# Layer-norm statistics of one slab moved to VectorE and of another to an earlier time on ScalarE, with their transposes at the head of the gate steps

## The chip, the cores and the metric

One core of a Trainium2 chip. The metric is device time of one execution in microseconds (us), median over runs on the chip. The span in a profile is about 1.8 us shorter than that time (185.5 against 187.29 in the first profile), because it runs from the first to the last instruction. The 193.67 of the kernel before is slow.

The engines: PE is the tensor engine (PEld its weight loads), DVE is VectorE, ACT is ScalarE, POOL is GpSimd, SP is the engine whose queue issues most transfers.

## The reference, cut to what matters

```python
xn = layernorm(x)                       # x: 2048 tokens x 512, bf16
h[t] = Lam_bar * h[t-1] + B_bar @ xn[t] # complex state of 512
s = 2 * Re(C @ h) + xn * Dskip
g = silu((gelu(xn @ w_gate) * (xn @ w_up)) @ w_down)   # hidden width 1376
out = x + s * g
```

## The kernel before

The 2048 tokens are four slabs of 512. For each slab PE computes eleven gate/up steps (`ffn`), then the scan's input for the next slab (`u_pair`, twice), then four tiles of the down projection (`down`). The products of the state with C (`y_mm`) for slab s are woven into the gate steps of slab s+1. The scan with its rotations runs on VectorE. PE needs the normalised input transposed; for slabs 1 to 3 ScalarE normalises a tile and a transposing transfer turns it:

```python
def ln_act(s, m):                       # statistics on ScalarE: sum and sum of squares
    for i, f in enumerate((AF.Copy, AF.Square)):
        junk = work.tile([P, D], BF16, name="junk", tag="junk", bufs=1)
        ACT(out=junk[:], in_=x_tok[:, s * M + m, :], func=f, accum_out=sx[:, s, i, m : m + 1])

def ln_out(s, m):                       # normalise on ScalarE, transpose by transfer
    xn = work.tile([P, D], BF16, name="xn", tag="xn", bufs=4)
    ACT(out=xn[:], in_=x_tok[:, s * M + m, :], func=AF.Identity, scale=rs[...], bias=nb[...])
    nc.sync.dma_start_transpose(out=xnT[:, :, c0 : c0 + P], in_=xn[:])

def epi(s, m, y_ps, g2):                # output tile: two VectorE operations, then the store
    ...
    nc.sync.dma_start(out=out_td[mg : mg + P, :], in_=ot[:])
```

Transposes and stores share one queue, SP's, which issues in program order. The order in slabs 1 and 2:

```python
if s < NS - 1:
    if j < M:           ln_act(s + 1, j)       # gate steps 0..3: statistics
    if j == M - 1:      ln_small(s + 1)        # four small VectorE ops, two on GpSimd
    if 5 <= j < 5 + M:  ln_out(s + 1, j - 5)   # gate steps 5..8: normalise and transpose
if j in Y_AT:                                  # Y_AT = (5, 7, 9, 10): y product and store
    m = Y_AT.index(j)
    epi(s - 1, m, y_mm(s - 1, m, hsts[s - 1]), g2s[s - 1, m])
```

The prologue, which turns out to matter for reading the times, runs idle matmuls (`dummies`) until the first normalised tiles are there:

```python
dummies(9)
nc.tensor.transpose(pt_ps[:, :], pv[:, :], ident[0:16, 0:16])
dummies(5)
...
tps = [t_xn0(0, xs[0]), t_xn0(1, xs[1])]       # first real work of PE
```

## Time and profile before

| | kernel before |
|---|---|
| runs ahead of the change | 187.57, 188.12, 193.67 us |
| profiled run | 187.29 us, span 185.5 us |
| PE busy | 178.7 us (96%) |
| VectorE busy | 151.6 us (82%) |
| ScalarE busy | 116.0 us (63%) |
| PE waits after 8.5 us | one, of 0.6 us |

How to read it: busy shares say which engine to look at; the waits say what it stood for; the chain says which of those stretches add up to the span. PE at 96% with one listed wait leaves little room. The lines are in the prediction below.

### The profile page before, as it was taken

What the parts mean: (1) busy time and instruction counts of PE and PEld (TensorE: products, weight loads), DVE (VectorE), ACT (ScalarE), POOL (GpSimd) and SP (SyncE); (2) the same over time, 40 slices, a digit from 0 to 9 for tenths busy, and PEclk for the clock granted to TensorE, in tenths of its full rate; (3) what the DMA queues carried; (4) which work ended last, traced back from release to release, by engine and by line L of the source; (5) the groups of instructions that cost most, each with busy time, mean ns of one, the idle gap of its engine ahead of it and who ended that gap; (6) DMA issues with size and microseconds to landing.
All of it is one profiled execution on the core that took longest, in us unless ns stands there. A gap on an engine that the chain in (4) does not pass through costs nothing.

```text
span 185.5 us, 2504 instructions
## 1 busy us (share of the span) xinstructions
PE 178.7 (96%) x887; PEld 85.8 (46%) x903; DVE 151.6 (82%) x233; ACT 116.0 (63%) x212; POOL 23.8 (13%) x42
## 2 busy tenths in 40 slices
PE   7899999999999999999999999989999999999992
PEld 2564444444444445444444444544444444554452
DVE  4877999999996699999999999999999993332034
ACT  3299996678899996376269949547329633441210
POOL 3679606200000110000000040000000000000000
PEclk9999999999999999999999999999999999999999
DMA  5996834895000013200000003300000000000001
GB/s 150 315 314 102 228 68 88 242 241 194 0 0 0 0 34 82 57 28 28 0 4 0 0 0 88 84 31 30 0 0 0 4 0 28 28 32 30 28 28 57
DMA packets 24444, 12.26 MB, mean 66 GB/s; under 512 B 15760, under 2 KB 24432, under 8 KB 24432
## 3 DMA queue, kind: packets, MB, share of 16 engines
q1 hardware_dynamic: 24256, 12.03, 25.8%
q8 instruction: 7, 0.11, 0.3%
q10 hardware_dynamic: 176, 0.07, 0.1%
q14 instruction: 5, 0.04, 0.1%
HBM read 6.33 MB, written 2.10 MB: 45 GB/s over the span
## 4 chain that ended last, share of the span: by engine, by line
PE 84%; ACT 6%; DVE 4%; DMA 3%; issue 1%; POOL 0%
PE f_ps L471 20%; PE up_ps L226 18%; PE g_ps L226 17%; PE u_ps L371 13%; PE y_ps L486 13%; ACT gt L459 2%; PE y_ps L491 2%; ACT ub L460 2%; DMA xnT<-xn 1%; DVE st L154 1%; DMA x_tok<-in_A_x_dram 1%; ACT xn L559 1%; PE y_ps L519 1%; DVE xn L165 1%; ACT L459 1%
## 5 line engine op out<-in xcount | busy, mean ns | idle before, releaser
L226 PE MATMUL g_ps<-xnT,wg 128*128 128x512 bf16 (+2 forms) x179 | 44.8, 369 | 0.8 <-ACT xnT L195 0.7
L226 PE MATMUL up_ps<-xnT,wu 128*128 128x512 bf16 (+2 forms) x181 | 45.2, 370 | 0.3
L471 PE MATMUL f_ps<-wd,at 128*128 128x512 bf16 (+1 forms) x172 | 38.5, 379 | 0.2
L459 ACT ACTIVATE gt<-g_ps 128x512 bf16<-128x512 f32 (+1 forms) x44 | 26.6, 605 | 11.6 <-PE g_ps L226 9.3
L460 ACT ACTIVATE ub<-up_ps 128x512 bf16<-128x512 f32 (+1 forms) x44 | 26.8, 610 | 4.3 <-PE up_ps L226 4.3
L417 DVE TENSOR_TENSOR_SCAN Ft<-rho,it,Wt 128x512 bf16<-128x512 f32 x24 | 29.3, 1266 | 0.0
L371 PE MATMUL u_ps<-xnT,BT 128*128 128x512 bf16 x127 | 28.4, 379 | 0.7 <-DMA xnT<-xn 0.6
L486 PE MATMUL y_ps<-C,hst 128*128 128x512 bf16 x117 | 28.2, 379 | 0.2
L226 PEld LDWEIGHTS <-wu 128*128 128x128 bf16 (+1 forms) x184 | 18.3, 100 | 19.7
L471 PEld LDWEIGHTS <-at 128*128 128x128 bf16 (+1 forms) x176 | 17.1, 98 | 20.6
L226 PEld LDWEIGHTS <-wg 128*128 128x128 bf16 (+1 forms) x184 | 17.8, 100 | 18.4 <-issue 0.8
L376 ACT ACTIVATE U<-u_ps 128x512 bf16<-128x512 f32 x32 | 19.0, 616 | 11.6 <-PE u_ps L371 11.6
L476 ACT ACTIVATE g<-f_ps 128x512 f32<-128x512 f32 x16 | 9.6, 597 | 22.6 <-PE f_ps L471 22.6
L504 DVE TENSOR_TENSOR yg<-y_ps,g 128x512 bf16<-128x512 f32 x15 | 10.2, 682 | 14.1 <-PE y_ps L491 10.3
L464 DVE TENSOR_TENSOR at<-gt,ub 128x1024 bf16<-128x1024 bf16 x20 | 13.7, 684 | 9.8 <-ACT ub L460 9.8
L371 PEld LDWEIGHTS <-BT 128*128 128x128 bf16 x128 | 12.4, 98 | 15.5 <-issue 0.9
L486 PEld LDWEIGHTS <-hst 128*128 128x128 bf16 x120 | 11.7, 98 | 13.6
L554 POOL TENSOR_TENSOR rs<-sx,mhalf 128x4 f32<-128x4 f32 x2 | 3.2, 1594 | 72.6 <-DVE sx L551 42.2
L559 ACT ACTIVATE xn<-x_tok,nb,rs 128x512 bf16<-128x512 bf16 x12 | 10.2, 849 | 2.9 <-POOL nb L555 2.9
L391 DVE TENSOR_TENSOR Wt<-pp,qq 128x1024 bf16<-128x1024 bf16 x16 | 10.5, 688 | 0.3
L391 DVE TENSOR_TENSOR hst<-pp,qq 128x1024 bf16<-128x1024 bf16 x16 | 10.4, 686 | 0.2
L387 DVE TENSOR_TENSOR pp<-U,cos_b 128x2048 bf16<-128x2048 bf16 x8 | 9.8, 1222 | 0.7 <-ACT U L376 0.4
(106 smaller groups left out, 159.8 us busy)
## 6 DMA issues: line engine op xcount, KB each, us to landing
out_dram<-ot SPq DMA_DIRECT2D x15, 128.0 KB, 1.7
x_tok<-in_A_x_dram SPq DMA_DIRECT2D x3, 512.0 KB, 6.6
wd<-in_B_w_down_dram SPq DMA_DIRECT2D x1, 1280.0 KB
wg<-in_B_w_gate_dram SPq DMA_DIRECT2D x1, 640.0 KB
wu<-in_B_w_up_dram SPq DMA_DIRECT2D x1, 640.0 KB, 8.6
wg<-in_B_w_gate_dram SPq DMA_DIRECT2D x1, 384.0 KB, 3.7
wu<-in_B_w_up_dram SPq DMA_DIRECT2D x1, 384.0 KB
wg<-in_B_w_gate_dram SPq DMA_DIRECT2D x1, 352.0 KB
```

The costliest lines, as they stand in the source:

```text
L226: nc.tensor.matmul(ps[:fs, a:b], lhsT=w[:, kt, fsl], rhs=xnT[:, kt, s * TS + a : s * TS + b], start=(kt == 0), stop=(kt == KT - 1),)
L371: nc.tensor.matmul(u_ps[:, :], lhsT=BT[:, ri, kt, pt * P : (pt + 1) * P], rhs=xnT[:, kt, cols], start=(kt == 0), stop=(kt == KT - 1),)
L376: ACT(out=U[:, ri, q, :], in_=u_ps[:, :], func=AF.Copy)
L391: return lambda: TT(out=dst()[i], in0=box["pp"][:, i, :, :], in1=box["qq"][:, 1 - i, :, :], op=op)
L417: nc.vector.tensor_tensor_scan(out=box["F"][:, ri, q, :], data0=rho[:, pt : pt + 1].to_broadcast([P, TS]), data1=box["W"][:, ri, q, :], in ...
L459: ACT(out=gt[:fs, i, :], in_=g_ps[:fs, :], func=AF.Gelu_apprx_tanh)
L460: ACT(out=ub[:fs, i, :], in_=u_ps[:fs, :], func=AF.Copy)
L464: dve(now() + 0.9, 0.61, lambda: TT(out=at[:, j - 1 : j + 1, :], in0=gt[:], in1=ub[:], op=ALU.mult))
L471: nc.tensor.matmul(f_ps[:, :], lhsT=at[:fs, k, m0 : m0 + P], rhs=wd[:fs, k, :], start=(k == 0), stop=(k == NFT - 1))
L486: nc.tensor.matmul(y_ps[:, :], lhsT=hst[:, j // NPT, j % NPT, m0 : m0 + P], rhs=C2[:, j // NPT, j % NPT, :], start=(j == 0), stop=False,)
L504: TT(out=yg[:], in0=y_ps[:, :], in1=g2[:], op=ALU.mult)
L559: ACT(out=xn[:], in_=x_tok[:, s * M + m, :], func=AF.Identity, scale=rs[:, s, m : m + 1], bias=nb[:, s, m : m + 1])
```

## The change

The intent: take the statistics passes of slabs 2 and 3 out of ScalarE's gate steps. Slab 2's go to VectorE, which has idle time early in slab 0; slab 3's stay on ScalarE but move under slab 1's down projection. The transposes can then go into gate steps 1 to 4. Slab 2's input is loaded earlier for this. A copy in the prologue is split over two engines, and the gate products are placed a little later in VectorE's order.

```diff
     load_gu(1)
+    load_x(2)
...
-    xnT_out(nc.scalar, 1, tps[1])
+    xnT_out(nc.scalar, 1, tps[1], 0, KT // 2)
+    xnT_out(nc.vector, 1, tps[1], KT // 2, KT)
...
+        lag = 0.9 + (2.5 if s == 0 else 0.5)
-            dve(now() + 0.9, 0.61, lambda: TT(out=at[:, j - 1 : j + 1, :], ...))
+            dve(now() + lag, 0.61, lambda: TT(out=at[:, j - 1 : j + 1, :], ...))
...
+    dve(13.0, 2.8, lambda: ln_vector(2))
...
+                if j == 3:
+                    ln_vector_small(2)
...
-                    for x in range(2, NS):
-                        load_x(x)
+                    load_x(3)
...
-                if s < NS - 1:
-                    if j < M:
-                        ln_act(s + 1, j)
-                    if j == M - 1:
-                        ln_small(s + 1)
-                    if 5 <= j < 5 + M:
-                        ln_out(s + 1, j - 5)
+                if s < NS - 1 and 1 <= j < 1 + M:
+                    ln_out(s + 1, j - 1)
...
+                if s == 1:
+                    ln_act(3, m)
+            if s == 1:
+                ln_small(3)
```

More of the change, by code (lines that the diff above doesn't have):

```diff
@@ L191, with xnT_out @@
     ACT(out=pf[:], in_=pt_ps[:, :], func=AF.Copy)
-    def xnT_out(eng, m, tp):
-        o = xnT[:, :, m * P : (m + 1) * P]
+    def xnT_out(eng, m, tp, k0=0, k1=KT):
+        o = xnT[:, k0:k1, m * P : (m + 1) * P]
         if eng is nc.scalar:
-            ACT(out=o, in_=tp[:, :, :], func=AF.Copy)
+            ACT(out=o, in_=tp[:, k0:k1, :], func=AF.Copy)
         else:
-            eng.tensor_copy(out=o, in_=tp[:, :, :])
+            eng.tensor_copy(out=o, in_=tp[:, k0:k1, :])
     bn(0, 0)
@@ L460, in ffn @@
         ACT(out=ub[:fs, i, :], in_=u_ps[:fs, :], func=AF.Copy)
+        lag = 0.9 + (2.5 if s == 0 else 0.5)
         if j == NFT - 1:
-            dve(now() + 0.9, 0.34, lambda: TT(out=at[:fs, j, :], in0=gt[:fs, 0, :], in1=ub[:fs, 0, :], op=ALU.mult))
+            dve(now() + lag, 0.34, lambda: TT(out=at[:fs, j, :], in0=gt[:fs, 0, :], in1=ub[:fs, 0, :], op=ALU.mult))
         elif i:
-            dve(now() + 0.9, 0.61, lambda: TT(out=at[:, j - 1 : j + 1, :], in0=gt[:], in1=ub[:], op=ALU.mult))
+            dve(now() + lag, 0.61, lambda: TT(out=at[:, j - 1 : j + 1, :], in0=gt[:], in1=ub[:], op=ALU.mult))
     def down(s, m, at):
@@ L566, with ln_vector, ln_vector_small @@
     hsts, ats, g2s = {0: hst0}, {0: at0}, {}
-    def ln1_stats():
+    G = nc.gpsimd
+    def ln_vector(x):
         for m in range(M):
-            bn(1, m)
+            bn(x, m)
         for m in range(M):
-            bn_end(1, m)
-    dve(10.3, 2.8, ln1_stats)
-    G = nc.gpsimd
-    ve1 = consts.tile([P, M], FP32, name="ve1")
-    G.tensor_scalar(out=ve1[:], in0=mv[:, 1, :, 1], scalar1=EPS, scalar2=None, op0=ALU.add)
-    G.tensor_tensor(out=rs[:, 1, :], in0=ve1[:], in1=mhalf[:], op=ALU.pow)
-    G.tensor_tensor(out=nb[:, 1, :], in0=mv[:, 1, :, 0], in1=rs[:, 1, :], op=ALU.mult)
-    G.tensor_scalar(out=nb[:, 1, :], in0=nb[:, 1, :], scalar1=-1.0, scalar2=None, op0=ALU.mult)
+            bn_end(x, m)
+    def ln_vector_small(x):
+        G.tensor_scalar(out=vx[:, x, :], in0=mv[:, x, :, 1], scalar1=EPS, scalar2=None, op0=ALU.add)
+        G.tensor_tensor(out=rs[:, x, :], in0=vx[:, x, :], in1=mhalf[:], op=ALU.pow)
+        G.tensor_tensor(out=nb[:, x, :], in0=mv[:, x, :, 0], in1=rs[:, x, :], op=ALU.mult)
+        G.tensor_scalar(out=nb[:, x, :], in0=nb[:, x, :], scalar1=-1.0, scalar2=None, op0=ALU.mult)
+    vx = consts.tile([P, NS, M], FP32, name="vx")
+    dve(10.0, 2.8, lambda: ln_vector(1))
+    ln_vector_small(1)
+    dve(13.0, 2.8, lambda: ln_vector(2))
     later(14.0, 1.2, lambda: TT(out=v4(t2_[:]), in0=v4(sa[:]), in1=sB, op=ALU.mult))
```

## The prediction

> **What bounds the kernel now.** I read the summary and the slices first, then what the tensor engine (PE) waited for, then the chain of waits, then time lines of the engines that the chain names.
>
> ```profile
> PE 178.7 (96%) x887; PEld 85.8 (46%) x903; DVE 151.6 (82%) x233; ACT 116.0 (63%) x212; POOL 23.8 (13%) x42
> ...
> PE   7899999999999999999999999989999999999992
> ...
> DVE  4877999999996699999999999999999993332034
> ```
>
> PE is full in every slice except the first two, the last one and one near two thirds. VectorE is nearly as full up to slice 33, so work added to it has to fit real gaps. Busy shares cannot tell whether PE runs at its own rate, so I take the rate from the chain: four 128x512 matmuls take 0.86 us, 0.216 us each.
>
> ```profile
> PE w_ps L146 <- DVE halfpi L122: 1.2, 1, 1.2
> PE g_ps L226 <- ACT xnT L195: 0.7, 1, 0.7
> PE u_ps L371 <- DMA xnT<-xn: 0.6, 1, 0.6
> PE tp L174 <- DVE xn L165: 0.2, 1, 0.2
> ```
>
> These are all of PE's waits (total, times, longest). Three lie before 8.5 us; the only later one is the 0.6 us, for a transposing transfer of the normalised input. The chain shows where it falls:
>
> ```profile
> 118.08 0.67 PE up_ps L226 x4
> 118.74 2.48 DMA xnT<-xn
> 121.22 0.25 issue
> 121.47 3.61 PE u_ps L371 x16
> ```
>
> (start, duration, what). Slab 3's projection into the scan cannot start until its last transpose lands; other PE work, a y product, covers all but 0.58 us of the 2.7 us. As a check, what must run from 9.90 us to the last matmul at 182.2: 336 gate/up matmuls, 128 for u, 176 for down and 120 for y, 760 x 0.2157 = 163.9; plus 16 half-width ones in 1.76, 60 small y ones in 3.3 and the split last y tile in 2.0. Sum 171.0 of 172.3 us elapsed. Of the rest 0.58 is that wait and about 0.7 is scattered pieces of 0.05 us called "issue". PE bounds the kernel; little besides that wait is in reach.
>
> Why was the transpose late? The store queue's time line and ScalarE's tell:
>
> ```profile
> 111.19 1.20 SPq L561 DMA_TRANSPOSE xnT<-xn  x1
> 113.12 0.33 SPq L508 DMA_DIRECT2D out_dram<-ot  x1
> 113.55 2.52 SPq L561 DMA_TRANSPOSE xnT<-xn  x2
> 118.32 0.33 SPq L508 DMA_DIRECT2D out_dram<-ot  x1
> 118.74 1.19 SPq L561 DMA_TRANSPOSE xnT<-xn  x1
> ```
>
> ```profile
> 110.35 0.81 ACT L559 ACTIVATE xn<-x_tok,nb,rs 128x512 bf16<-128x512 bf16 x1 [2.62 <-POOL nb L555]
> ```
>
> ScalarE got the statistics late (2.62 us idle, on GpSimd), and the fourth transpose stood behind a store whose data VectorE finished only at 118.3. ScalarE had written its tile by about 116.2.
>
> **What the Trainium skill says.** "TensorE: Matmul & The Clock Gate", Step-by-step, gives a back-to-back gap of about 216 ns for N=512; the trace agrees (0.2157). Its section Back-to-back issue gap reports 131 ns as a sustained figure; this trace shows no such pace, and the measurement decides. The same page, Architectural detail, says that ScalarE's and VectorE's queues are strict FIFO; the trace agrees as far as it shows, since idle time stands in front of instructions whose input is late. So the order of issue, which this change moves, matters. "PSUM — Partial Sum Buffer", Terms, says two engines must not touch one bank and quadrant at once, reads included. No run here shows a collision; it bears on the split copy below.
>
> **The change, part by part**, with the listing of each engine's instruction order.
>
> *Removed under the gate steps.* In slabs 1 and 2 ScalarE loses four pairs of statistics passes each. A pass starts about 0.76 us after the one before, so each slab loses 8 x 0.76 = 6.1 us there. PE did not wait for them (its pace in 50.7 to 118 is the floor), so this alone is worth nothing.
>
> *Transposes first.* In the new order all four transposes of slabs 2 and 3 stand ahead of the four stores. They follow gate steps 1 to 4: ScalarE needs 2 x 0.48 + 0.70 = 1.66 us a step against PE's 1.73. Slab 3's should be issued by about 106 and landed by 110, 11 us before 121. **Gain 0.58 us.**
>
> *Slab 3's statistics under slab 1's down projection.* ScalarE has gaps of 1.78 us there between Silus; two passes take 1.5, so three pairs are hidden. The last pair pushes the Gelu table load and the first Gelu from 96.3 to about 97.4. PE has eight accumulator banks and at 1.73 us a step would need the first one back only near 101. Cost 0. VectorE's four small operations wait for the last pair, until about 96.2; by my count below VectorE arrives at about 96.1.
>
> *Slab 2's statistics on VectorE.* Four at 0.60 spacing plus four aggregates, 2.74 to 2.83 us. They now follow slab 1's, which end at 12.77.
>
> ```profile
> 12.41 0.36 DVE L157 BATCH_NORM_AGGREGATE mv<-st 128x2 f32<-128x6 f32 x4
> 14.59 0.69 DVE L464 TENSOR_TENSOR at<-gt,ub 128x1024 bf16<-128x1024 bf16 x1 [1.82 <-ACT ub L460]
> ...
> 18.34 0.71 DVE L464 TENSOR_TENSOR at<-gt,ub 128x1024 bf16<-128x1024 bf16 x1 [0.70 <-ACT ub L460]
> ...
> 21.68 0.69 DVE L464 TENSOR_TENSOR at<-gt,ub 128x1024 bf16<-128x1024 bf16 x1 [0.18 <-ACT ub L460]
> ```
>
> The gaps total 1.82 + 0.70 + 0.18 = 2.70 us, about the cost, but the data are late. Slab 2's 0.52 MB load stands behind the second up-weight load, issued at 4.34 and landing 8.6 us later, at 12.94; at 315 GB/s (slices 1 and 2) it needs 1.7 us more: 14.6. So the statistics run 14.7 to 17.5, the nine operations to the first rotation need 9.25 us back to back, and the rotation starts at 26.75 instead of 24.72: **VectorE is 2.0 us late**. It then has no gap until slab 1. Walking on with trace durations, scans and coefficient folds interleaved, each fold after its ScalarE input, the slab-0 state that the first y product needs is done at about 59.1. PE needs it at 61.05. Slack 2.0 us; cost on the path 0. Down projection 0 needs the last product at 41.2; it moves from 37.3 to 39.3. In slab 1 VectorE then fills gaps of 1.47, 0.98 and 0.51, and by 83 should be about 1.2 us ahead of before.
>
> *Split copy in the prologue.* PE waits 0.69 us for ScalarE's 0.60 us copy (6.93 to 7.53). The new code halves it, but the listing shows VectorE's half waiting on ScalarE's, which fits the bank rule. Estimate: a small ScalarE operation takes 0.19 us, a 512-wide one 0.60, so a half takes 0.40; then VectorE's half, about 0.25, ends near 7.6. The first half of each product may start 0.15 earlier. But at 9.90 PE waits on VectorE's copy, finished at 9.85 at the end of a VectorE run that starts at 7.61 and is not shortened. So the gain is swallowed there; the inserted copy may even push that run back by up to 0.1. **Net 0 to -0.1 us.**
>
> Sum: 0.58 - 0.05 = about 0.5 us gained of 188.1.
>
> **Rivals.** (1) *VectorE late to the first y product.* If slab 2's input lands after about 16.6, the 2.0 us slack is used up and each further microsecond is one of PE idle; transfers overlapped in 12 to 14 us (DMA share 1.3), so 15.5 is possible, 17 hardly. It would turn -0.5 into up to +1. (2) *The load delays the B transposes.* They go back by up to 1.7 us; the first landed near 11 and is needed at 18.56, the fourth is issued at 11.3, lands some 3.7 later, near 15, and is needed at 21.1. Even so 3 us are left. (3) *Freed ScalarE makes PE faster.* Against it: PE is at 0.216 us per matmul throughout and waits only once. A gain of 2% would need 3.8 us, and all waits and scattered pieces after 9.9 us amount to 1.3. (4) *Rescheduled products (longer lag) hold gate buffers.* There are three pairs; the first product moves from 14.6 to 17.5, and the fourth pair needs its buffer at 24.1. Free.
>
> **Range and chances.** The median before is 188.12; its fast runs are 187.57 and 188.12 and the profiled one 187.29, so run scatter (0.8 us) exceeds the effect. From their middle, about 187.7, less 0.5 gives 187.2 us. Down to 186.2: the gain and good runs; up to 188.6: rival 1 or poor runs. Slower by 2% needs over 3.7 us of new stalls, which only a badly late load would give.
>
> **What would show it.** Right: no PE wait on the transposing transfer; slab 3's four transposes issued before 108 with the stores after them; VectorE idle on the slab 2 input near 12.8 until 14.6; the first rotation near 26.7; PE's pace unchanged; the first Gelu of slab 2 about 1 us later; the full-rate run of PE still starting near 9.9. Wrong: a new PE wait on a VectorE state at 61, on a B transpose near 18.6, or on an accumulator bank near 101; or PE's full rate starting earlier than 9.7, which would mean that the split gained after all.

## The result, and the profile after

| | before | changed |
|---|---|---|
| median, same rounds | 187.57 us of the fast runs (187.33, 187.57, 188.12); 187.84 with the slow 193.67 | 186.54 us (186.40 to 186.74) |
| ratio of fast runs | | 0.994, 95% interval 0.9912 to 0.9969 |
| profiled span | 185.5 us | 184.9 us |

A ratio here is the mean time of one kernel's fast runs over that of the other's fast runs of the same rounds, so it is not quite the ratio of the medians. At a bar of 2% the verdict is "same"; the gain of about half a percent is clear of zero.

PE's waits in the changed kernel (total us, times, longest us):

```profile
PE w_ps L147 <- DVE halfpi L123: 1.2, 1, 1.2
PE g_ps L228 <- ACT xnT L196: 0.5, 1, 0.5
PE up_ps L228 <- DMA wu<-in_B_w_up_dram: 0.3, 1, 0.3
```

The wait for the transposing transfer is gone. A new one of 0.3 us, for the first up-projection weights, stands at 8.5 us. SP's time line in the changed kernel:

```profile
57.31 6.21 SPq L564 DMA_TRANSPOSE xnT<-xn  x4
65.10 15.04 SPq L511 DMA_DIRECT2D out_dram<-ot  x4
100.38 6.22 SPq L564 DMA_TRANSPOSE xnT<-xn  x4
```

Four transposes, then four stores, as foreseen: slab 3's are issued by 106.6.

VectorE's time line (a bracket is idle time and what ended it):

```profile
14.74 2.47 DVE L155 BATCH_NORM_STATS2 st<-x_tok 128x6 f32<-128x512 bf16 x4 [1.84 <-DMA x_tok<-in_A_x_dram]
...
26.38 1.22 DVE L389 TENSOR_TENSOR pp<-U,cos_b 128x2048 bf16<-128x2048 bf16 x1
...
57.23 1.28 DVE L393 TENSOR_TENSOR hst<-pp,qq 128x1024 bf16<-128x1024 bf16 x2
```

The added statistics wait for slab 2's input until 14.74 (14.6 was predicted), the first rotation starts at 26.38 (26.75), and slab 0's state is done at 58.5 (59.1). PE never waits on VectorE after the prologue.

**Where the time came from.** PE's time line in front of the two u projections, before:

```profile
77.09 0.39 PE L491 MATMUL y_ps<-diagI,xnT 128*128 128x128 bf16 x4
77.52 2.75 PE L371 MATMUL u_ps<-xnT,BT 128*128 128x512 bf16 x12
...
120.50 0.39 PE L491 MATMUL y_ps<-diagI,xnT 128*128 128x128 bf16 x4
121.47 2.75 PE L371 MATMUL u_ps<-xnT,BT 128*128 128x512 bf16 x12 [0.58 <-DMA xnT<-xn]
```

and in the changed kernel:

```profile
77.48 0.39 PE L494 MATMUL y_ps<-diagI,xnT 128*128 128x128 bf16 x4
77.70 2.54 PE L373 MATMUL u_ps<-xnT,BT 128*128 128x512 bf16 x11
...
120.69 0.39 PE L494 MATMUL y_ps<-diagI,xnT 128*128 128x128 bf16 x4
120.92 1.46 PE L373 MATMUL u_ps<-xnT,BT 128*128 128x512 bf16 x6
```

Read the first column, not the bracket. The profile does not see when a matmul ends; it models the end. Four small matmuls take 0.39 us from the first start to the last modelled end, but at full pace the next group starts 0.22 us after they start (77.48 to 77.70). Before, the spacing was 0.43 in slab 1 and 0.97 in slab 2. So PE lost 0.43 - 0.22 = 0.21 us in front of slab 2's projection, which no wait of PE showed, and 0.97 - 0.22 = 0.75 us in front of slab 3's, of which the bracket showed 0.58. Together **0.96 us**. The first loss has a trace on the weight-load row of the kernel before, without a named cause:

```profile
77.49 2.50 PEld L371 LDWEIGHTS <-BT 128*128 128x128 bf16 x13 [0.18 <-issue]
```

SP's time line of the kernel before shows what stood there:

```profile
74.34 0.36 SPq L508 DMA_DIRECT2D out_dram<-ot  x1
74.79 1.20 SPq L561 DMA_TRANSPOSE xnT<-xn  x1
```

Slab 2's fourth transpose was issued behind a store at 74.79. The transposes around it took 2.4 to 2.5 us from issue to landing, so it landed near 77.3 (an estimate), and the projection started at 77.52. In slab 3 the landing at 121.22 was likewise followed by the projection at 121.47. It is the same stall, only shorter.

The span fell by only 0.6 us in this pair of profiles, because PE's unbroken full-rate work began 0.4 us later in the second. I mark as the **start** of a run the moment when PE begins the third group of half-width gate matmuls, the first work that needs the third and fourth tiles of slab 0. It is 9.90 before and 10.30 in the changed kernel. Time minus start is 187.29 - 9.90 = 177.39 and 186.74 - 10.30 = 176.44: 0.95 us apart. Whether the start differs by chance is for the experiments.

### The profile page after: what moved, and what is told of

Its sections match the earlier page's. It is cut to its first block, busy times and chain, and to the rows that moved or that the text cites. A ratio compares the mean times of both kernels' runs of the same rounds, so it can differ in the third digit from the quotient of the medians.

```text
span 184.9 us, 2493 instructions
## 1 busy us (share of the span) xinstructions
PE 178.8 (97%) x887; PEld 86.0 (46%) x903; DVE 154.3 (83%) x238; ACT 111.9 (61%) x196; POOL 20.6 (11%) x44
## 4 chain that ended last, share of the span: by engine, by line
PE 93%; DMA 3%; SPq 1%; issue 1%; DVE 0%
PE up_ps L228 21%; PE f_ps L474 20%; PE g_ps L228 20%; PE u_ps L373 15%; PE y_ps L489 14%; DMA wu<-in_B_w_up_dram 3%; PE y_ps L494 2%; PE y_ps L522 1%; SPq L89 1%; SPq L96 0%; PE tp L175 0%; DVE yg L532 0%; DVE ot L533 0%; PE y_ps L528 0%
## 5 line engine op out<-in xcount | busy, mean ns | idle before, releaser
L461 ACT ACTIVATE gt<-g_ps 128x512 bf16<-128x512 f32 (+1 forms) x44 | 27.1, 616 | 20.4 <-PE g_ps L228 16.9
L462 ACT ACTIVATE ub<-up_ps 128x512 bf16<-128x512 f32 (+1 forms) x44 | 27.3, 620 | 6.7 <-PE up_ps L228 6.4
L373 PEld LDWEIGHTS <-BT 128*128 128x128 bf16 x128 | 12.5, 98 | 14.6
L155 DVE BATCH_NORM_STATS2 st<-x_tok 128x6 f32<-128x512 bf16 x12 | 7.6, 682 | 3.6 <-DMA x_tok<-in_A_x_dram 3.6
```

Source lines behind the costliest of these rows:

```text
L373: nc.tensor.matmul(u_ps[:, :], lhsT=BT[:, ri, kt, pt * P : (pt + 1) * P], rhs=xnT[:, kt, cols], start=(kt == 0), stop=(kt == KT - 1),)
L461: ACT(out=gt[:fs, i, :], in_=g_ps[:fs, :], func=AF.Gelu_apprx_tanh)
L462: ACT(out=ub[:fs, i, :], in_=u_ps[:fs, :], func=AF.Copy)
```

## The experiments

All outputs are right. e1 and e2 repeat the two kernels unaltered. Medians are of the fast runs; ratios are to the kernel before in the same rounds. "Time - start" is from the profiled run of each.

| kernel | median us | range | ratio (95%) | start | time - start |
|---|---|---|---|---|---|
| before (first profile) | | | | 9.90 | 177.39 |
| e1 before, again | 187.70 | 187.40-187.89 | 1.0003 (0.9985-1.002) | 10.31 | 177.37 |
| changed (first profile) | 186.54 | 186.40-186.74 | 0.994 (0.9912-0.9969) | 10.30 | 176.44 |
| e2 changed, again | 186.66 | 186.42-186.96 | 0.9951 (0.9934-0.9968) | 10.04 | 176.41 |
| e3 no split copy | 186.66 | 186.54-186.95 | 0.9952 (0.9936-0.9967) | 10.10 | 176.44 |
| e4 before, stores behind | 186.92 | 186.43-187.18 | 0.996 (0.9942-0.9978) | 10.74 | 176.44 |
| e5 changed, transposes late | 186.53 | 186.31-187.26 | 0.9946 (0.9928-0.9963) | 10.36 | 176.44 |
| e6 statistics three times | 188.18 | 187.79-188.37 | 1.0024 (1.0003-1.0045) | 9.98 | 178.19 |
| e7 three idle matmuls | 186.42 | 186.35-186.56 | 0.9934 (0.992-0.9949) | 10.03 | 176.43 |
| e8 prologue reordered | 186.50 | 186.17-187.24 | 0.9942 (0.9922-0.9963) | 10.28 | 176.43 |
| e9 statistics twice | 186.52 | one run | none | 10.07 | 176.45 |
| e11 e4 with e8's prologue | 186.44 | 186.37-186.88 | 0.9933 (0.9911-0.9954) | 10.44 | 176.44 |
| e12 one idle matmul | 187.76 | 186.32-188.35 | 0.9988 (0.9955-1.0021) | 9.91 | 176.41 |

The last column is the main finding. The two profiles of the kernel before give 177.37 and 177.39; ten others lie between 176.41 and 176.45; only e6 stands apart. All other scatter of the profiled runs sits in the start.

### e1 and e2: both kernels again

No edit.

> The kernel before, unaltered, to see how far its own runs and profiles scatter. Theory A (the extra gain is real and comes from two late transposes): ratio to itself 1.000 within 0.3%; in its profile the fresh projection of slab 2 starts 0.43 us after the last four small y products start (0.22 at pace, so 0.21 lost) and that of slab 3 0.97 us after (0.75 lost), in every profile. Theory B (the gain beyond 0.5 us is scatter of the load of the first weights): these two losses stay, but the moment at which the tensor engine reaches its full rate moves by several tenths of a microsecond between profiles, 9.9 in the first one.

> The changed kernel, unaltered. Theory A: ratio 0.994 to 0.996, both losses in front of the projections of slabs 2 and 3 gone (0.22 us spacing); the 0.3 us wait on the first up-projection weights at 8.5 us is chance and is smaller or gone in this profile, with the span then near 184.6. Theory B: ratio 0.996 to 0.998. If the wait on the first weights is there again with the same size, the added load causes it.

Measured: the kernel before shows the same two losses within 0.02 us (0.41 and 0.96 us spacing), while its start moved from 9.90 to 10.31. The changed kernel has 0.23 us in both places. Its wait for the first up weights is gone, so it comes by chance and not from the added load; e11 below, which loads slab 2's input at the old place, had one of 0.4 us. With more runs (6, against 11 of the kernel before) the ratio is 0.9951: 0.92 us. The interval of this ratio, up to 0.9968, still reaches into what theory B expected. It is the spacings and the time minus the start that decide for theory A; what theory B said of the moving start is true as well. The first comparison's 0.994, 1.12 us, is more than the 0.96 us found in the traces; luck of the starts is the likely reason, but the starts of its other runs were not seen.

### e3: without the split copy

```diff
-    xnT_out(nc.scalar, 1, tps[1], 0, KT // 2)
-    xnT_out(nc.vector, 1, tps[1], KT // 2, KT)
+    xnT_out(nc.scalar, 1, tps[1])
```

> The changed kernel with the copy of the second transposed tile given back to ScalarE whole. Theory (from the prediction): the split is worth nothing or slightly less, so the time is the changed kernel's within 0.15 us, or up to 0.1 us better, and VectorE's normalisation of the third tile starts at 7.6 instead of 7.74. Rival: the split is what brought the unexpected half microsecond; then this is 0.3 to 0.6 us slower than the changed kernel.

Measured: the same median, 186.66. The split neither gains nor costs. Why, is on VectorE's time line of the changed kernel:

```profile
6.76 0.17 DVE L161 TENSOR_SCALAR ve<-mv 128x2 f32<-128x2 f32 x1
6.84 0.42 DVE L198 COPY xnT<-tp 128x512 bf16<-128x512 bf16 x1
7.47 0.29 DVE L198 COPY xnT<-tp 128x256 bf16<-128x256 bf16 x1 [0.22 <-ACT xnT L196]
7.74 0.74 DVE L166 TENSOR_SCALAR xn<-x_tok,mv,rs 128x512 bf16<-128x512 bf16 x2
```

The half copy waits for ScalarE's half and ends just as the next operation may start. That operation comes 0.98 us after the `ve` line here, and also 0.98 us after it without the split (6.63 to 7.61 before, 6.78 to 7.76 in e3), because it waits on GpSimd. My expectation that it would come 0.13 earlier without the split was wrong: the whole run of operations had merely started later.

### e4: only the store order

The kernel before; the stores of the first two output tiles are kept back until the fourth transpose has been queued. Compared trace against trace, the operations of PE, VectorE, ScalarE and GpSimd stand in the same order; only SP's queue differs.

```diff
-        nc.sync.dma_start(out=out_td[mg : mg + P, :], in_=ot[:])
+        stores.append(lambda: nc.sync.dma_start(out=out_td[mg : mg + P, :], in_=ot[:]))
...
                     epi(s - 1, m, y_mm(s - 1, m, hsts[s - 1]), g2s[s - 1, m])
+                if s == NS - 1 or j >= 8:
+                    store_now()
```

> The kernel before with one thing altered: the stores of the first two output tiles of a slab are issued behind the four transposes of the next slab. All compute engines keep their order; statistics stay where they were. Theory A (the late transposes are all of it, and the reason that they are late is the store in front): both losses (0.21 and 0.75 us) vanish, time 0.95 us under before, ratio 0.995, equal to the changed kernel's. Rival (the statistics' late arrival on ScalarE is what makes the transposes late): the fourth transpose still cannot go before ScalarE has written its tile at about 116.2, and a wait of some tenths stays; ratio 0.998 or more.

Its SP queue and its PE in front of slab 3's projection:

```profile
112.01 6.20 SPq L566 DMA_TRANSPOSE xnT<-xn  x4
118.31 6.83 SPq L509 DMA_DIRECT2D out_dram<-ot  x3
```

```profile
121.14 0.39 PE L492 MATMUL y_ps<-diagI,xnT 128*128 128x128 bf16 x4
121.36 2.97 PE L372 MATMUL u_ps<-xnT,BT 128*128 128x512 bf16 x13
```

The spacing is 0.22 in both places and time - start is 176.44, exactly the changed kernel's. No statistics were moved, and the whole gain is there. With the stores out of the way the transposes are early enough. The ratio, 0.996, looks weaker than 0.9951, but the intervals overlap; the profiled run, the slowest of the six, started at 10.74, and the starts of the others were not seen. None of the change's other edits (the earlier load, the later gate products) is in e4, so they add nothing that time minus start shows; neither was tested alone.

### e5: the changed kernel with its transposes at the old place

```diff
-                if s < NS - 1 and 1 <= j < 1 + M:
-                    ln_out(s + 1, j - 1)
+                if s < NS - 1 and 5 <= j < 5 + M:
+                    ln_out(s + 1, j - 5)
```

> The changed kernel with the normalised tiles and their transposes back at gate steps 5 to 8, so that transposes and stores interleave in the store queue as before; only the statistics are moved. Theory (a store in front is harmful only when its data are late; with the statistics gone from between, VectorE finishes the second output tile near 115 and ScalarE its fourth tile near 114): the fourth transpose of slab 3 is issued near 115, lands near 117.5, three microseconds before it is needed; no loss, time that of the changed kernel within 0.15 us. Rival (the early place of the transposes is what counts): 0.2 to 0.95 us slower than the changed kernel, with the spacing in front of slab 3's projection over 0.22 again.

Its SP queue:

```profile
114.94 0.33 SPq L511 DMA_DIRECT2D out_dram<-ot  x1
115.37 1.20 SPq L564 DMA_TRANSPOSE xnT<-xn  x1
```

The store still stands in front of the fourth transpose, but VectorE is earlier and the store leaves at 114.9 instead of 118.3. The transpose is issued at 115.4, over five microseconds before its data are needed at 121. Time - start is 176.44. So stores behind the transposes (e4), or the changed kernel without its early transposes (e5), is each enough by itself; together they remove the same 0.96 us once. What in e5 made VectorE's second output tile ready at 114.9 was not separated: the statistics are moved, and the later gate products change VectorE's order too.

### e6 and e9: how much room the added VectorE work had

```diff
-    dve(13.0, 2.8, lambda: ln_vector(2))
+    dve(13.0, 2.8, lambda: [ln_vector(2) for _ in range(3)])   # e9: range(2)
```

> The changed kernel with slab 2's statistics on VectorE computed three times over (same result): 5.5 us more of VectorE work in slab 0, to measure how much room the added work had. Theory (VectorE's work in slab 0 is on the path only past a room of some 2.7 us): the last product of slab 0 comes near 44.3 and stops the first down projection by 0.9 us, the state of slab 0 comes near 63.1 and stops the first y product by about 1.2; in sum 2.1 us slower than the changed kernel (1.6 to 2.8). Rival 1 (VectorE is the bound throughout): 5.5 us slower. Rival 2 (all of it hidden): no slower.

> The changed kernel with slab 2's statistics on VectorE computed twice (same result), 2.65 us more VectorE work. From the run with three times: its last product of slab 0 comes at 44.9, 1.7 us after the tensor engine wanted it. One repetition less is 2.65 us earlier, 42.2 against 43.3: no wait at all. Time minus the moment at which full rate starts is then 176.4 us, the changed kernel's figure. Rival (any added VectorE work costs something): 0.3 us or more above that.

Measured: three times costs 178.19 - 176.43 = 1.76 us, twice costs nothing. PE in the run with three:

```profile
41.09 2.32 PE L474 MATMUL f_ps<-wd,at 128*128 128x512 bf16 x10
44.97 7.52 PE L474 MATMUL f_ps<-wd,at 96*128 96x512 bf16 x34 [1.56 <-DVE at L465]
```

The whole cost lies in the down projection, which waits for slab 0's last product: ten matmuls at 0.2157 would have ended at 43.25, the next starts at 44.97, 1.72 us later. The y product, for which I had expected another 1.2 us, did not wait at all: it started at 62.69 while the last quarter of the state (the imaginary parts of its second half) was written only at 63.48. Its first six matmuls do not read that quarter; the seventh does, 1.3 us later, at 63.98. Without the 1.72 us that PE had already lost, the seventh would have come at 62.26, 1.2 us before its data: the first wait covered the second. So the sum of 1.76 us lies in the expected range of 1.6 to 2.8 partly by luck, for its two parts were to be 0.9 and 1.2. In the changed kernel the last product is ready at 39.66 and wanted about 43.6, so VectorE's work had some 4 us of room there. For the y product the room is much the same: the state is done at 58.51, and the seventh matmul comes at 61.27 + 1.29 = 62.56. The prediction gave about 2 for both.

### e7, e8, e11, e12: the start

e7 has three idle matmuls after the small transpose in place of five. e8 adds to that the whole copy of e3 and puts VectorE's copy of the third tile ahead of two small operations. e11 is e4 with e8's idle matmuls and copy order. e12 is e8 with one idle matmul.

```diff
-    dummies(5)
+    dummies(3)          # e12: dummies(1)
...
+    xnT_out(nc.vector, 2, tps[2])        # e8, e11, e12
     TSC(out=kr[:], in0=ang[:], scalar1=MAGIC, ...)
     TT(out=ang[:], in0=ang[:], in1=kr[:], op=ALU.subtract)
-    xnT_out(nc.vector, 2, tps[2])
```

> The changed kernel with three idle matmuls in place of five after the first small transpose. Theory (the tensor engine's clock rises at a moment that differs from run to run; where it rises late, the idle matmuls at half rate stand in front of the first real transposes and move everything after by up to 0.8 us): the slowest runs improve, the spread of the runs shrinks, the median falls by 0.1 to 0.3 us. Rival (the idle matmuls are needed for the clock to rise): it rises later, slower by 0.1 us or more.

> Changed kernel, without the split copy, with three idle matmuls, and with VectorE's copy of the third transposed tile put ahead of two small angle operations. Theory: the tensor engine's second wait in the prologue (for that copy, until 9.9) goes, full rate starts at 9.6 to 9.8 in good runs, median 186.2 to 186.4. Rival (the angles' delay of 0.35 us runs through ScalarE, which is busy without gaps from 10 to 26 us): no gain, a new wait of the tensor engine on an accumulator bank before 26 us.

> The kernel before with the two stores issued behind the transposes, three idle matmuls and the third tile's copy moved ahead; no statistics moved. Theory (stores and prologue are all there is): as fast as the changed kernel with the same prologue, median 186.2 to 186.6, time minus start of full rate 176.4. Rival (the moved statistics help elsewhere): 0.2 us or more above.

> The prologue version with one idle matmul in place of three. Theory (in runs in which the clock rises late the idle matmuls delay the first transposes): the slow runs of the three-matmul version (186.7 to 187.2) come down to 186.4 or so and the fast ones (186.2) stay. Rival (the activity is needed): the clock rises later in some runs, slow runs of 187 and more stay or get worse.

What moves the start is seen on PE's time line. The five idle matmuls and the first transposes in the first profile of the kernel before:

```profile
4.76 1.25 PE L146 MATMUL w_ps<-warm 128*128 128x512 bf16 x5
6.18 0.72 PE L174 MATMUL tp<-ident,xn 128*128 128x128 bf16 x8 [0.17 <-DVE xn L165]
```

and in e4, with the same instructions:

```profile
5.25 2.17 PE L146 MATMUL w_ps<-warm 128*128 128x512 bf16 x5
7.26 0.61 PE L174 MATMUL tp<-ident,xn 128*128 128x128 bf16 x8
```

In e4 all fourteen idle matmuls ran at about 0.43 us each, half rate, and the first transposes, whose first tile VectorE had ready by about 6.3, waited behind them until 7.26. In the first run the rate had doubled before the second batch. The Trainium skill, "TensorE: Matmul & The Clock Gate", Part 1: The HAM clock gate, says that the array's clock rises only after a window of activity of some 3.4 us that runs freely, so that the moment differs from run to run. The traces agree that the moment differs from run to run. From the spacing of the idle matmuls, which begin at 1.17 us, I put the rise (an estimate) near 4.1 us in the first run, near 3.8 in e6 and past 7 in e4. That is 2.7 us after the first matmul in e6 and more than 6 in e4, so the length of 3.4 us does not come out of these traces. The clock is not all: in the first profile of the changed kernel and in e11 the wait for the up weights, 0.33 and 0.40 us, is part of a late start.

Results: e7's five fast runs lie within 0.21 us and have the lowest median, but its interval overlaps the changed kernel's, and e8 and e11, with three idle matmuls too, spread over 1.07 and 0.51 us; a smaller scatter is not shown. e8 has the fastest single runs (186.17, 186.18), yet also 187.24; its median of 186.50 is outside the expected 186.2 to 186.4. The profiled start, 10.28, is late because the idle matmuls ended only at 6.50. Its groups at 9.84 and 10.28 follow at pace, but so do those of e1 and e4, which have the old copy order and started late as well; that PE's second prologue wait is gone is seen in e12, whose early groups at 9.47 and 9.91 follow at pace, where the kernel before had 9.34 and 9.90. e11 is as fast as anything that contains the moved statistics, again with 176.44. e12 refutes my theory that fewer idle matmuls are better: its runs reach 188.35 and its median is back at 187.76. Its one profile fell in the fastest run (186.32), so that the clock rises later in the slow ones fits but was not seen. The listed clocks point that way: three of its four runs over 187 us list a mean granted clock of 0.989 to 0.990, the lowest of all fast runs (the others list 0.996 or more), but the fourth (187.66) lists 1.000. No version was shown to beat the changed kernel: e7 and e11 have medians 0.1 to 0.2 us lower, inside the intervals.

## Why the prediction was right or wrong, point by point

- **PE bounds the kernel, and little but the transpose wait is in reach:** right. The pace stayed at 0.216 us per 512-wide matmul and all that was gained is two waits on transposes. The total of what I called reachable, 1.3 us, was also right: 0.96 was lost time, and 0.34 of scattered pieces remain (in the changed kernel the matmuls from the start at 10.30 to the last end at 181.64 take 171.34, of which 171.0 is the work at pace).
- **Gain 0.58 us:** this is the mis-sized term of the sum. It was read from the idle column in front of the matmul. That column starts at the modelled end of the matmul before, so 0.17 us of the gap was hidden, and the smaller loss in front of slab 2's projection lay inside it but for 0.04 us, too little to be listed. Measured by spacing of starts it is 0.75 + 0.21 = 0.96 us. I had booked the missing 0.38 as "scattered pieces of 0.05 us".
- **Why the transpose was late:** the store in front was the right cause: e4 removes the loss by the order alone, with the statistics as late as before. It is the order together with the late data of the store, for in e5 the store still stands in front and nothing is lost.
- **ScalarE relieved, worth nothing by itself:** right in that PE's pace does not change. By way of the queue e5's early work helps, but there ScalarE and VectorE are both changed, and ScalarE's share is not shown.
- **Slab 3's statistics under the down projection, cost 0:** right. VectorE's small operations came at 96.0 (96.1) and the first Gelu of slab 2 at 97.6 (97.4), with no wait of PE near 101.
- **Slab 2's statistics on VectorE:** right in time (1.7 us late at the first rotation, 2.0 predicted) and in cost (none). The room was underestimated, about 4 us and not 2.0, because the prediction took the start of the down projection and of the y product for the moment at which the last data are needed; e6 shows that the eleventh matmul of the one and the seventh of the other need them. e9's doubled statistics cost nothing (one run).
- **Split copy, net 0 to -0.1:** right at 0 (e3). VectorE's half did wait for ScalarE's (0.22 us), as the listing of orders had shown. One sign failed: the start was to stay near 9.9 and was 10.30, with a wait of 0.33 for the up weights in front of it; e1 shows the unaltered kernel at 10.31, so scatter alone reaches as far.
- **Rivals 1, 2 and 4:** none occurred. Rival 3's bound of 1.3 us held.
- **The number:** 187.2 predicted, 186.54 measured, inside the range. Of the difference of 0.66 us, 0.46 is the mis-sized gain (0.96 against 0.5); the rest, 0.2, is within the scatter of the runs.

## What to carry to other kernels

Measure a stall of the tensor engine by the spacing of starts against the spacing at pace: idle columns begin at a modelled end and hide short waits. When loads or transposes share an in-order queue with stores, look at what stands in front of the late one; reordering two stores gained here as much as moving the work of two engines. Before comparing runs for half a percent, subtract the moment at which full-rate work begins, unless the change itself moves it: it differed by 0.8 us between profiled runs with the same prologue, as much as the effect.

## What the Trainium skill lacked or had wrong

- "TensorE: Matmul & The Clock Gate", Back-to-back issue gap: it gives 131 ns per matmul as the sustained figure for N=512. In every run here streams of weight load and matmul after the prologue kept to 0.2157 us, which is the figure that it calls the isolated gap.
- The same page, Part 1: it says that the warm-up is under 1% of a kernel. That holds here, but it lacks a warning for comparisons of half a percent: the start moved from 9.90 to 10.74 us between profiled runs with the same prologue, 0.45% of the time and as large as the change studied, where five idle matmuls queued ahead of real work took 1.25 us in one run and 2.17 in the other.
- "Perfetto Trace Analysis", Tensor Engine Instruction: it says that a matmul's end is an estimate, but not what follows for idle time. Here a 0.75 us loss was listed as 0.58 and one of 0.21 us was not listed as a wait of PE at all.
- No page that I found times the statistics operation on VectorE: 0.677 us for a 128x512 bf16 tile, one every 0.60 us back to back.
